# Retention, experts and a cosine MLP in one kernel: the places of tokens in stages of one chunk each, with the column comparison on POOL

## The chip, the cores and the metric

The kernel runs on one core of a Trainium2 chip. The metric is the time of one execution in microseconds (us) on the device; several runs are given by their median. The engines are called as in the profile: PE is TensorE, DVE is VectorE, ACT is ScalarE, POOL is GpSimd, SP is SyncE, which issues most of the transfers.

## What is computed

The batch is 8, with 8 heads, 576 positions and a head size of 64, so 4608 tokens of 512 numbers. All is float32.

```python
# retention: q, k, v are (8, 8, 576, 64)
scores = q @ k^T / 8
ret = scores * where(rel >= 0, gamma[h] ** rel, 0)      # rel = row - column
x = (ret @ v), heads put side by side                   # 4608 x 512
# mixture of 8 experts, one per token
logits = x @ w_gate                                     # 512 x 8
e = argmax(logits);  gate = softmax(logits)[e]          # sum + 1e-9
y = gate * (relu(x @ w1[e]) @ w2[e])                    # 1024 wide
# MLP with a cosine gate
h = y @ w_in                                            # 2048 wide
out = (h * cos(h)) @ w_out
```

## The kernel before

The kernel has three stages: retention together with the routing of the tokens, then the experts one after the other on the tokens gathered for each, then the MLP. The change is in the first stage alone.

The first stage goes through 40 steps, one chunk of a sequence each (`steps`, `CH`: four chunks of 128 tokens and one of 64 for each of the 8 sequences). The recording is manual: each engine executes its instructions in the order in which the program's text issues them. One pass of the loop over `i` (L497 on) issues work of several steps:

- `transposes(i + 1)`, `scores(i)`, `decay_k(i + 2)`, then in passes 20 to 27 `unit_split`, which splits one half unit of expert 0's weights into two parts on ACT and DVE (its load was issued two passes earlier by `unit_load`),
- `inter(i - 1)` and `intra(i - 1)`: the product with the carried state, the product of masked scores (`pT`) and v, the state's update,
- `table` for the groups that are due, `place` for the group that was routed in the pass before, `rows(i - 2)`, and `route` where a group is complete,
- the loads of step `i + 4` on SP, behind the store of the rows (`xd`).

`rows` (L335) makes the tokens' rows and the router's logits in one product, copies the rows on ACT and reduces the logits (`lgt`) on DVE at L344. Its PSUM tile has the tag of the scores' tile, "sc", in a pool with one buffer:

```python
two = ps1.tile([P, 8, P], F32, tag="sc", name="sc")     # L290, scores
two = ps1.tile([P, 8, P], F32, tag="sc", name="rw")     # L338, rows (then rearranged)
```

So the scores of the next step wait until `lgt` has read the tile, and the products of `rows` wait until both halves of `pT` have.

The routing works on groups of chunks (`groups`, L476): five chunks for each of the first seven sequences, and 2, 1 and 2 for the last. `route` (L351) finds each token's expert: five small DVE instructions. `place` (L369) does all that follows but the table: the ranks of the tokens within their experts by small products on PE with `rsb`, the counts so far; the slot `dst`; a comparison of the slot with the first slot of each of the 40 columns of 128 slots (`dd`, `ge`, `hot`, L396 to L401); the slot within its column (`rm`); one-hot rows over 128 slots (`oh`) and three rows of values (`rt`) on POOL; the gates (`gates`); and the new counts (`rsum`, `rsb`). `ve` is POOL, or DVE for the last group (`last`). `table` (L450) adds products of `oh` and `rt` to a table in SBUF that lists the tokens of each slot. It follows `place` by two passes.

Of the kernel before, what the change touches and what calls it, by code (L numbers as in the profile page):

```python
# [11 lines left out]
F32 = mybir.dt.float32  # L12
# [5 lines left out]
ALU = mybir.AluOpType  # L18
AX = mybir.AxisListType
# [3 lines left out]
P = 128  # L23
# [3 lines left out]
E = 8  # L27
# [3 lines left out]
CH = [(0, 128), (128, 128), (256, 128), (384, 128), (512, 64)]  # L31
# [72 lines left out]
def attn_moe_kernel(ctx, tc, q, k, v, wg, w1, w2, win, wout, ctab, out):  # L104
    nc = tc.nc
# [22 lines left out]
    rsum = cp.tile([P, E], F32, name="rsum")  # L128
# [19 lines left out]
    SL = E * NBLK  # L148
# [43 lines left out]
    with ExitStack() as actx:  # L192
        ap1 = actx.enter_context(tc.tile_pool(name="ap1", bufs=1))
        ap2 = actx.enter_context(tc.tile_pool(name="ap2", bufs=2))
# [12 lines left out]
        rsb = ap1.tile([P, E], BF16, name="rsb")  # L207
# [39 lines left out]
        steps = [(b, c) for b in range(B) for c in range(NCH)]  # L247
# [87 lines left out]
        def rows(i):  # L335
            b, c = steps[i]
            o, n = CH[c]
            two = ps1.tile([P, 8, P], F32, tag="sc", name="rw").rearrange("p (j a) t -> p j (a t)", a=2)  # L338
            for j in range(4):
                mm(out=two[:, j, 0:RW], lhsT=xts[i % 3][:, j, :], rhs=wgi[:, j, :], start=(j % 2 == 0), stop=True,  # L340
                   skip_group_check=True)
            x = ap3.tile([P, 4, P], F32, tag="xs", name="xs")
            nc.scalar.copy(out=x[:n], in_=two[:n, :, 0:P])
            nc.vector.tensor_reduce(out=lgt[b % 2][:n, c, :], in_=two[:n, :, P:RW].rearrange("p j e -> p e j"),  # L344
                                    axis=AX.X, op=ALU.add)
            nc.sync.dma_start(out=xd[b * SEQ + o:b * SEQ + o + n, :], in_=x[:n].rearrange("p j t -> p (j t)"))
# [22 lines left out]
        def place(i0, n, ohb, df):  # L369
            c0 = steps[i0][1]  # L370
            sh = [P, n, E]
            ex = ap2.tile(sh, F32, tag="ex", name="ex")
# [9 lines left out]
            for c in range(n - 1):  # L382
                m = n - 1 - c
                mm(out=rk[:, c + 1:, :], lhsT=ones, rhs=ohb[:, c, :].unsqueeze(1).to_broadcast([P, m, E]),
                   start=False, stop=(c == n - 2), skip_group_check=True)
            last = i0 + n == NS
            t1 = ap2.tile(sh, F32, tag="t1", name="t1")
            nc.vector.tensor_mul(out=t1, in0=rk, in1=ohb)
            dst = dsts[:, i0:i0 + n]
            nc.vector.tensor_reduce(out=dst, in_=t1, axis=AX.X, op=ALU.add)  # L390

            ve = nc.vector if last else nc.gpsimd
            hs = [P, n, SL]
            lo = cc(C_LO, SL).unsqueeze(1).to_broadcast(hs)
            dd = ap2.tile(hs, F32, tag="dd", name="dd")
            nc.vector.tensor_tensor(out=dd, in0=dst.unsqueeze(2).to_broadcast(hs), in1=lo, op=ALU.subtract)  # L396
            ge = ap2.tile(hs, F32, tag="ge", name="ge")
            nc.vector.tensor_scalar(out=ge, in0=dd, scalar1=0.0, scalar2=None, op0=ALU.is_ge)
            hot = ap2.tile(hs, F32, tag="hot", name="hot")
            nc.vector.scalar_tensor_tensor(out=hot, in0=dd, scalar=float(P), in1=ge, op0=ALU.is_lt, op1=ALU.mult)  # L400
            ve.tensor_tensor(out=dd, in0=dd, in1=hot, op=ALU.mult)  # L401
            rm = ap2.tile([P, n], F32, tag="rm", name="rm")
            nc.vector.tensor_reduce(out=rm, in_=dd, axis=AX.X, op=ALU.add)
            rt = ap2.tile([P, n, 3, SL], F32R, tag="rt", name="rt")
# [4 lines left out]
            for c in range(n):  # L409
                ve.tensor_scalar(out=oh[:, c, :], in0=cc(C_IOTA, P), scalar1=rm[:, c:c + 1], scalar2=None,  # L410
                                 op0=ALU.is_equal)
# [14 lines left out]

            if not last:
                gates()
            if n > 2:
                rr = ap2.tile([P, E], F32, tag="rr", name="rr")  # L430
                nc.vector.tensor_reduce(out=rr, in_=ohb[:, :n - 1].rearrange("p c e -> p e c"), axis=AX.X, op=ALU.add)
                nc.vector.tensor_add(out=rsum, in0=rsum, in1=rr)
            elif n == 2:
                nc.vector.tensor_add(out=rsum, in0=rsum, in1=ohb[:, 0, :])
            m = CH[c0 + n - 1][1]
            nc.vector.tensor_add(out=rsum[:m], in0=rsum[:m], in1=ohb[:m, n - 1, :])
            nc.vector.tensor_copy(out=rsb, in_=rsum)

            def enter(k0, k1):
                w = (k1 - k0) * SL  # L440
# [26 lines left out]
        groups[NS - 3] = (NS - 3, 1)  # L467
        groups[NS - 1] = (NS - 2, 2)
        routed = []
        tabled = []  # L470

        load(0, "q")
# [22 lines left out]
        for i in range(NS + 5):  # L495
            if i + 1 < NS:
                transposes(i + 1)  # L497
            if i < NS:
                scores(i)
            if i + 2 < NS:  # L500
                decay_k(i + 2)
            if 20 <= i < 20 + len(wq):
                unit_split(*wq[i - 20], upA)
            if i == 0:
                setup()
            if 1 <= i <= NS:
                inter(i - 1)
                intra(i - 1)

            prev, waiting[:], tabled[:] = waiting[:], tabled[:], []  # L510
            for r in prev:
                table(*r)
            if i >= NS + 2:
                while waiting:
                    table(*waiting.pop(0))
            prev, routed[:] = routed[:], []
            for r in prev:
                place(*r)
            if 0 <= i - 2 < NS:
                rows(i - 2)  # L520
            if i - 2 in groups:
                route(*groups[i - 2])
            if i + 4 < NS:
                loads(i + 4)
            if 18 <= i < 18 + len(wq):
                unit_load(ap3, *wq[i - 18])

        assert not tabled and not routed and not waiting
        assert not tabled and not routed
        rp = ps2.tile([P, 512], F32, tag="x", name="xps")  # L530
        mm(out=rp[:, :E], lhsT=ones, rhs=rsb, start=True, stop=True)
# [503 lines left out]
```

## Time and profile before

| | |
|---|---|
| time, median of 3 runs | 1568.36 us (1565.32 to 1570.71) |
| the profiled execution: time, span | 1571.7 us, 1569.8 us |
| mean granted clock of PE | 0.971 |
| PE busy | 1502.7 us, 96% of the span |
| DVE, ACT, POOL busy | 896.1, 781.1, 359.3 us |
| stage one | the first 291 us or so of the span |

The times of the rows further down are in us from the start of the span. A row of the timeline merges like instructions that follow each other ("x16" is their number), and in square brackets stands the idle time of the engine ahead of them, with what ended it. The granted clock is a share of 2.4 GHz: 1.00 is that level, 0.50 is the lower one of 1.2 GHz, and a value between is a mean over the stretch.

### The profile page before, as it was taken

To read this page: it belongs to the slowest core of one execution; us is meant where nothing else is said; L and a number is where in the kernel's file an instruction comes from. 1 tells how busy PE (TensorE), PEld (TensorE's weight loads), DVE (VectorE), ACT (ScalarE), POOL (GpSimd) and SP (SyncE) were. 2 spreads that over 40 slices of the span, in tenths; PEclk is the share of its full clock that TensorE was granted. 3 is DMA by queue.
4 is the path that set the end of the run, shared out by engine and by line. 5 is a ranking of instruction groups with operands and counts; after the bars stand their busy time and mean duration, and the time that the engine had idled before them with its cause. 6 is when DMAs were issued, how large, how long until landed. Compare 5 with 4: busy or idle time off the path is not lost.

```text
span 1569.8 us, 24472 instructions
## 1 busy us (share of the span) xinstructions
PE 1502.7 (96%) x9565; PEld 1334.4 (85%) x9565; DVE 896.1 (57%) x1618; ACT 781.1 (50%) x1395; POOL 359.3 (23%) x399
## 2 busy tenths in 40 slices
PE   8997798799999999999999999999999999999998
PEld 7887788699999999999878888888888888888886
DVE  3555655556575665652256656666665656666554
ACT  3334332244445445433266666666565666666654
POOL 3111111365666657562000101010000101010101
PEclk9999899699999999999999999999999999999999
DMA  9768763365657556556640100000010100000000
GB/s 184 161 146 186 182 136 88 104 203 190 201 188 226 195 182 237 180 162 213 218 162 28 48 7 34 21 27 28 1 53 1 54 1 28 0 27 1 28 0 27
DMA packets 168520, 163.10 MB, mean 104 GB/s; under 512 B 119012, under 2 KB 127664, under 8 KB 166352
## 3 DMA queue, kind: packets, MB, share of 16 engines
q1 hardware_dynamic: 155696, 110.50, 25.8%
q0 software_dynamic: 10688, 36.31, 6.6%
q10 hardware_dynamic: 2016, 14.68, 2.8%
q8 instruction: 76, 1.25, 0.3%
q14 instruction: 44, 0.36, 0.1%
HBM read 115.70 MB, written 45.76 MB: 103 GB/s over the span
## 4 chain that ended last, share of the span: by engine, by line
issue 42%; PE 4%; POOL 2%; ACT 1%; DVE 1%; DMA 0%; POOLq 0%; SPq 0%
PE hps L907 2%; POOL out_dram L959 2%; PE acc L949 1%; PE acc L951 1%; PE acc L950 1%; DVE sa L918 0%; ACT ka L915 0%; DVE sa L919 0%; ACT sa L921 0%; ACT sa L922 0%; POOL spare L140 0%; DVE ka L917 0%; DMA yin<-ydT 0%; ACT sa L923 0%; DVE gl L934 0%
## 5 line engine op out<-in xcount | busy, mean ns | idle before, releaser
L907 PE MATMUL hps<-yT,wunit 128*128 128x512 f32 x1728 | 417.5, 391 | 0.4 <-ACT yT L894 0.4
L907 PEld LDWEIGHTS hps<-yT,wunit 128*128 128x128 f32 x1728 | 324.9, 188 | 69.8 <-DVE yT L895 1.3
L949 PE MATMUL acc<-wunit,gh 128*128 128x512 f32 x576 | 224.1, 389 | 0.0
L950 PE MATMUL acc<-wunit,gh 128*128 128x512 f32 x576 | 224.1, 389 | 0.0
L951 PE MATMUL acc<-wunit,gl 128*128 128x512 f32 x576 | 224.1, 389 | 0.0
L621 PE MATMUL hps<-hh,wunit 128*128 128x360 f32 (+1 forms) x1024 | 223.6, 310 | 0.0
L606 PE MATMUL hps<-xT,wunit 128*128 128x360 f32 (+1 forms) x1536 | 222.8, 306 | 0.5 <-ACT xT L591 0.5
L606 PEld LDWEIGHTS hps<-xT,wunit 128*128 128x128 f32 x1536 | 220.6, 190 | 1.2 <-ACT xT L591 0.9
L959 POOL DMA_INDIRECT out_dram<-orow,perm x36 | 35.2, 978 | 808.7 <-DVE orow L955 802.3
L929 DVE TENSOR_TENSOR sa<-hps,sa 128x512 f32<-128x512 f32 x144 | 99.3, 690 | 160.2 <-ACT sa L923 160.2
L921 ACT ACTIVATE sa<-sa 128x512 f32<-128x512 f32 x144 | 91.1, 633 | 193.8 <-DVE sa L919 193.8
L698 POOL TENSOR_TENSOR wunit<-wst,wunit 128x512 fp32r<-128x512 f32 x112 | 157.6, 1426 | 89.6 <-ACT wunit L697 89.4
L621 PEld LDWEIGHTS hps<-hh,wunit 128*128 128x128 f32 x1024 | 172.1, 192 | 0.0
L621 PE MATMUL hps<-hl,wunit 128*128 128x360 f32 (+1 forms) x512 | 158.1, 309 | 4.8 <-DVE hl L610 4.8
L610 DVE SCALAR_TENSOR_TENSOR hl<-hps,hh 128x360 fp32r<-128x360 f32 (+1 forms) x128 | 60.6, 474 | 178.1 <-ACT hh L609 178.1
L915 ACT ACTIVATE ka<-hps,biases 128x512 f32<-128x512 f32 x144 | 99.0, 688 | 69.4 <-PE hps L907 69.4
L951 PEld LDWEIGHTS acc<-wunit,gl 128*128 128x128 f32 x576 | 108.2, 188 | 22.5
L950 PEld LDWEIGHTS acc<-wunit,gh 128*128 128x128 f32 x576 | 108.1, 188 | 22.5
L949 PEld LDWEIGHTS acc<-wunit,gh 128*128 128x128 f32 x576 | 108.2, 188 | 22.4
L623 ACT COPY yev<-hps 128x256 f32<-128x256 f32 (+1 forms) x64 | 26.7, 417 | 169.1 <-issue 93.9
L923 ACT ACTIVATE sa<-sa,biases 128x512 f32<-128x512 f32 x144 | 104.1, 723 | 4.7
L917 DVE TENSOR_SCALAR ka<-ka 128x512 f32<-128x512 f32 x144 | 61.0, 424 | 74.2 <-ACT ka L915 74.2
(148 smaller groups left out, 2055.5 us busy)
## 6 DMA issues: line engine op xcount, KB each, us to landing
wst<-in_moe_w_dram SPq DMA_DIRECT2D x64, 512.0 KB, 4.5
wd<-cvo POOLq DMA_DIRECT2D x32, 512.0 KB, 3.9
wunit<-wd ACTq DMA_DIRECT2D x14, 1024.0 KB, 5.9
yin<-ydT SPq DMA_DIRECT2D x36, 256.0 KB, 2.7
ldq<-in_q_dram SPq DMA_DIRECT2D x32, 256.0 KB, 3.5
ldk<-in_k_dram SPq DMA_DIRECT2D x32, 256.0 KB, 4.2
ldv<-in_v_dram SPq DMA_DIRECT2D x32, 256.0 KB, 4.5
xd<-xs SPq DMA_DIRECT2D x32, 256.0 KB, 2.2
```

Source lines behind the costliest of these rows:

```text
L606: mm(out=ph[:, :n], lhsT=u[:, a, kc, f0:f0 + P], rhs=t[:, bq, kc, :n], start=(idx == 0), stop=(idx == 11))
L621: mm(out=py[:, :n], lhsT=u[:, w], rhs=t[:, :n], start=(fc == 0 and g == 0), stop=(fc == 7 and g == 2))
L698: nc.gpsimd.tensor_sub(out=u[:, 1, 2 * g + c], in0=s[:, c], in1=u[:, 0, 2 * g + c])
L907: mm(out=ph, lhsT=u[:, a, kc, f0:f0 + P], rhs=t[:, bq, kc, :], start=(idx == 0), stop=(idx == 11))
L915: nc.scalar.activation(out=ka, in_=ph, func=AF.Identity, scale=INV2PI, bias=magic)
L921: nc.scalar.activation(out=sa, in_=sa, func=AF.Sin, scale=0.5)
L923: nc.scalar.activation(out=sa, in_=sa, func=AF.Identity, scale=-2.0, bias=one)
L929: nc.vector.tensor_mul(out=sa, in0=ph, in1=sa)
L949: mm(out=a, lhsT=gh[:, s], rhs=u[:, 0, fc % 4], start=(fc == 0), stop=False)
L950: mm(out=a, lhsT=gh[:, s], rhs=u[:, 1, fc % 4], start=False, stop=False)
L951: mm(out=a, lhsT=gl[:, s], rhs=u[:, 0, fc % 4], start=False, stop=(fc == 15))
L959: ins = nc.gpsimd.indirect_dma_start(out=out[:, :], out_offset=bass.IndirectOffsetOnAxis(ap=perm[:, k:k + 1], axis=0), in_=o, in_offset=None)
```

## The change

`place` is cut in two. What is left in `place` is the ranks, the slot, the comparison and the new counts. The rest, from `rm` on, is a new function `spread`, with the gates in it. For a group that isn't the last, `spread` runs one pass later, and `table` so two passes after that. For the last group `place` calls it at once, in the old order.

For groups that aren't the last the comparison (`dd`, `ge`, `hot`) moves from DVE to POOL; the instruction that made `hot` becomes two there. In the loop, `rows` comes ahead of `spread` and `place`, and so does `route`.

```diff
@@ -393,12 +393,35 @@
             hs = [P, n, SL]
             lo = cc(C_LO, SL).unsqueeze(1).to_broadcast(hs)
             dd = ap2.tile(hs, F32, tag="dd", name="dd")
-            nc.vector.tensor_tensor(out=dd, in0=dst.unsqueeze(2).to_broadcast(hs), in1=lo, op=ALU.subtract)
+            ve.tensor_tensor(out=dd, in0=dst.unsqueeze(2).to_broadcast(hs), in1=lo, op=ALU.subtract)
             ge = ap2.tile(hs, F32, tag="ge", name="ge")
-            nc.vector.tensor_scalar(out=ge, in0=dd, scalar1=0.0, scalar2=None, op0=ALU.is_ge)
+            ve.tensor_scalar(out=ge, in0=dd, scalar1=0.0, scalar2=None, op0=ALU.is_ge)
             hot = ap2.tile(hs, F32, tag="hot", name="hot")
-            nc.vector.scalar_tensor_tensor(out=hot, in0=dd, scalar=float(P), in1=ge, op0=ALU.is_lt, op1=ALU.mult)
+            if last:
+                ve.scalar_tensor_tensor(out=hot, in0=dd, scalar=float(P), in1=ge, op0=ALU.is_lt, op1=ALU.mult)
+            else:
+                ve.tensor_scalar(out=hot, in0=dd, scalar1=float(P), scalar2=None, op0=ALU.is_lt)
+                ve.tensor_tensor(out=hot, in0=hot, in1=ge, op=ALU.mult)
             ve.tensor_tensor(out=dd, in0=dd, in1=hot, op=ALU.mult)
+            if last:
+                spread(i0, n, ex, hot, dd, True)
+            if n > 2:
+                rr = ap2.tile([P, E], F32, tag="rr", name="rr")
+                nc.vector.tensor_reduce(out=rr, in_=ohb[:, :n - 1].rearrange("p c e -> p e c"), axis=AX.X, op=ALU.add)
+                nc.vector.tensor_add(out=rsum, in0=rsum, in1=rr)
+            elif n == 2:
+                nc.vector.tensor_add(out=rsum, in0=rsum, in1=ohb[:, 0, :])
+            m = CH[c0 + n - 1][1]
+            nc.vector.tensor_add(out=rsum[:m], in0=rsum[:m], in1=ohb[:m, n - 1, :])
+            nc.vector.tensor_copy(out=rsb, in_=rsum)
+            if not last:
+                placed.append((i0, n, ex, hot, dd, False))
+
+        def spread(i0, n, ex, hot, dd, last):
+
+            c0 = steps[i0][1]
+            hs = [P, n, SL]
+            ve = nc.vector if last else nc.gpsimd
             rm = ap2.tile([P, n], F32, tag="rm", name="rm")
             nc.vector.tensor_reduce(out=rm, in_=dd, axis=AX.X, op=ALU.add)
             rt = ap2.tile([P, n, 3, SL], F32R, tag="rt", name="rt")
@@ -426,15 +449,6 @@
 
             if not last:
                 gates()
-            if n > 2:
-                rr = ap2.tile([P, E], F32, tag="rr", name="rr")
-                nc.vector.tensor_reduce(out=rr, in_=ohb[:, :n - 1].rearrange("p c e -> p e c"), axis=AX.X, op=ALU.add)
-                nc.vector.tensor_add(out=rsum, in0=rsum, in1=rr)
-            elif n == 2:
-                nc.vector.tensor_add(out=rsum, in0=rsum, in1=ohb[:, 0, :])
-            m = CH[c0 + n - 1][1]
-            nc.vector.tensor_add(out=rsum[:m], in0=rsum[:m], in1=ohb[:m, n - 1, :])
-            nc.vector.tensor_copy(out=rsb, in_=rsum)
 
             def enter(k0, k1):
                 w = (k1 - k0) * SL
@@ -467,6 +481,7 @@
         groups[NS - 3] = (NS - 3, 1)
         groups[NS - 1] = (NS - 2, 2)
         routed = []
+        placed = []
         tabled = []
 
         load(0, "q")
@@ -513,19 +528,22 @@
             if i >= NS + 2:
                 while waiting:
                     table(*waiting.pop(0))
-            prev, routed[:] = routed[:], []
-            for r in prev:
-                place(*r)
             if 0 <= i - 2 < NS:
                 rows(i - 2)
+            to_spread, placed[:] = placed[:], []
+            to_place, routed[:] = routed[:], []
             if i - 2 in groups:
                 route(*groups[i - 2])
+            for r in to_spread:
+                spread(*r)
+            for r in to_place:
+                place(*r)
             if i + 4 < NS:
                 loads(i + 4)
             if 18 <= i < 18 + len(wq):
                 unit_load(ap3, *wq[i - 18])
 
-        assert not tabled and not routed and not waiting
+        assert not tabled and not routed and not waiting and not placed
         assert not tabled and not routed
         rp = ps2.tile([P, 512], F32, tag="x", name="xps")
         mm(out=rp[:, :E], lhsT=ones, rhs=rsb, start=True, stop=True)
```

What the change moves, at three places. `ohb` is a token's expert as a one-hot row, `t` the ranks masked by it, `lg` the PSUM tile of ranks and table, `rw` the PSUM tile of `rows`.

DVE, first group of five chunks, from the middle of `place` to the next step's `pT`. Before:

```order
L403 TENSOR_REDUCE rm<-dd 128x5
L416 TENSOR_REDUCE gts<-ex 128x5
L417 TENSOR_SCALAR gts<-gts 128x5
L418 RECIPROCAL gts<-gts 128x5
L421 CAST gh<-gts 128x5
L422 TENSOR_TENSOR gl<-gts,gh 128x5
L431 TENSOR_REDUCE rr<-ohb 128x8
L432 TENSOR_TENSOR rsum<-rsum,rr 128x8
L436 TENSOR_TENSOR rsum<-rsum,ohb 64x8
L437 CAST rsb<-rsum 128x8
L344 TENSOR_REDUCE lgt_135<-rw 128x8
L299 TENSOR_TENSOR pT<-sc,ca 128x4x128 x2
```

Ahead of these stand L388, L390, L396, L398 and L400, which are t, dsts and the comparison. Now, from the end of the step's `intra`:

```order
L325 TENSOR_TENSOR xt_123<-xps,gx 128x512
L344 TENSOR_REDUCE lgt_135<-rw 128x8
L388 TENSOR_TENSOR t_728<-lg,ohb 128x40
L390 TENSOR_REDUCE dsts<-t_728 128x5
L410 TENSOR_REDUCE rr<-ohb 128x8
L411 TENSOR_TENSOR rsum<-rsum,rr 128x8
L415 TENSOR_TENSOR rsum<-rsum,ohb 64x8
L416 CAST rsb<-rsum 128x8
L299 TENSOR_TENSOR pT<-sc,ca 128x4x128 x2
```

`lgt` has moved from behind fifteen instructions of `place` to directly behind `xt`; the comparison has gone; rm and the gates (now L426 and L439 to L445) stand one step further down, behind the next `lgt` and ahead of the `pT` of the 64-token chunk.

POOL, one group of five chunks. Before:

```order
L401 TENSOR_TENSOR dd<-dd,hot 128x200
L406 TENSOR_SCALAR tokc<-ct 128x5
L407 TENSOR_TENSOR rt<-hot,tokc 128x5x40
L410 TENSOR_SCALAR oh<-ca,rm 128x128 x5
L424 TENSOR_TENSOR rt<-hot,gh 128x5x40
L424 TENSOR_TENSOR rt<-hot,gl 128x5x40
```

Now:

```order
L396 TENSOR_TENSOR dd<-dsts,ca 128x200
L398 TENSOR_SCALAR ge<-dd 128x200
L403 TENSOR_SCALAR hot<-dd 128x200
L404 TENSOR_TENSOR hot<-hot,ge 128x200
L405 TENSOR_TENSOR dd<-dd,hot 128x200
L429 TENSOR_SCALAR tokc<-ct 128x5
L430 TENSOR_TENSOR rt<-hot,tokc 128x5x40
L433 TENSOR_SCALAR oh<-ca,rm 128x128 x5
L447 TENSOR_TENSOR rt<-hot,gh 128x5x40
L447 TENSOR_TENSOR rt<-hot,gl 128x5x40
```

Four instructions on 128x200 have come ahead of the product that was POOL's first.

PE, the end of the stage, from the ranks of the group of one chunk to those of the last group; the rows of the difference, where L458 is the table's line L444 under its new number:

```order
 L380 LDWEIGHTS tri
 L380 MATMUL lg<-ohb,tri 128x8
-L340 MATMUL rw<-wgi,xt_127 128x136 x4
-L444 MATMUL lg<-rt,oh 128x120 x2
 L340 MATMUL rw<-wgi,xt_123 128x136 x4
-L444 MATMUL lg<-rt,oh 128x120
+L458 MATMUL lg<-rt,oh 128x120 x3
 L376 LDWEIGHTS ones
 L376 MATMUL lg<-rbase,ones 128x16
```

The rows of the last chunk but one go ahead of these ranks (further up), and the tables of the last two groups ahead of the last ranks stand together behind the products of the last rows.

In the steps with `place`, the products of `rows` (L340) also stand ahead of the rank products (L376 to L384) on PE, and on ACT the copy of the rows (L343) ahead of `ex` (L373). SP's order is unchanged, and so is all that follows the stage on every engine.

## Rows read from the trace of the kernel before

**Rows 1.** Two stretches of the attention stage. Columns: the stretch in us, its length, then the busy time and number of instructions of PE, weight loads, DVE, ACT and POOL, the granted clock, the mean busy share of the DMA engines, and GB/s.

```profile
84.00:117.00 33.00, 29.82 (x354) 26.90 (x352) 17.44 (x47) 10.55 (x25) 5.25 (x10) 0.90 0.63 144
...
153.00:191.00 38.00, 31.00 (x350) 27.98 (x349) 22.60 (x52) 15.47 (x29) 5.25 (x10) 0.87 0.82 192
```

**Rows 2.** The waits between 20 and 260 us: who waited for whom, us in total, how often, the longest.

```profile
DVE lgt L344 <- ACT xs L343: 32.4, 25, 1.8
PE sc L295 <- DVE lgt L344: 28.5, 12, 3.7
...
ACT wunit L179 <- DMA wst<-in_moe_w_dram: 14.2, 6, 4.8
```

**Rows 3.** PE's timeline: the scores (L295) of the seven steps that follow a `place` of five chunks, each with the products of `rows` (L340) that end its step, and a step without such a wait (249.05 to 254.77). Columns: start, length, engine, line, operation, tiles, shapes, number, and the idle time ahead.

```profile
57.11 1.83 PE L295 MATMUL sc<-qT,kpT 64*128 64x128 f32 x16 [3.05 <-DVE lgt L344]
...
62.37 1.19 PE L340 MATMUL rw<-wgi,xt 128*128 128x136 f32 x8
...
88.88 2.08 PE L295 MATMUL sc<-qT,kpT 64*128 64x128 f32 x16 [3.03 <-DVE lgt L344]
...
95.36 1.19 PE L340 MATMUL rw<-wgi,xt 128*128 128x136 f32 x8
...
121.86 1.74 PE L295 MATMUL sc<-qT,kpT 64*128 64x128 f32 x16 [3.02 <-DVE lgt L344]
...
127.08 1.19 PE L340 MATMUL rw<-wgi,xt 128*128 128x136 f32 x8
...
158.18 1.16 PE L295 MATMUL sc<-qT,kpT 64*128 64x128 f32 x16 [3.03 <-DVE lgt L344]
...
163.44 1.19 PE L340 MATMUL rw<-wgi,xt 128*128 128x136 f32 x8
...
196.29 1.16 PE L295 MATMUL sc<-qT,kpT 64*128 64x128 f32 x16 [3.03 <-DVE lgt L344]
...
201.54 1.19 PE L340 MATMUL rw<-wgi,xt 128*128 128x136 f32 x8
...
228.04 2.08 PE L295 MATMUL sc<-qT,kpT 64*128 64x128 f32 x16 [3.03 <-DVE lgt L344]
...
233.30 1.19 PE L340 MATMUL rw<-wgi,xt 128*128 128x136 f32 x8
...
249.05 1.17 PE L340 MATMUL rw<-wgi,xt 128*128 128x136 f32 x8
...
251.10 1.16 PE L295 MATMUL sc<-qT,kpT 64*128 64x128 f32 x16
...
254.77 0.19 PE L376 MATMUL lg<-rbase,ones 128*128 128x40 bf16 x1
...
259.79 2.08 PE L295 MATMUL sc<-qT,kpT 64*128 64x128 f32 x16 [3.02 <-DVE lgt L344]
...
266.17 1.19 PE L340 MATMUL rw<-wgi,xt 128*128 128x136 f32 x8
```

**Rows 4.** The timeline of DVE, and one row of POOL, around the seventh `place`: the step before it (250.86 to 252.31) and the `place` itself.

```profile
250.86 0.18 DVE L344 TENSOR_REDUCE lgt<-rw 64x8 f32<-64x32 f32 x1 [0.76 <-ACT xs L343]
...
252.01 0.20 DVE L366 TENSOR_TENSOR ohb<-rsc,m 128x40 bf16<-128x40 f32 x1
...
252.31 1.29 DVE L299 TENSOR_TENSOR pT<-sc,ca 128x512 f32<-128x512 f32 x2
...
255.14 0.20 DVE L388 TENSOR_TENSOR t<-lg,ohb 128x40 f32<-128x40 f32 x1
...
255.37 0.20 DVE L390 TENSOR_REDUCE dsts<-t 128x5 f32<-128x40 f32 x1
...
257.38 0.36 DVE L403 TENSOR_REDUCE rm<-dd 128x5 f32<-128x200 f32 x1 [0.72 <-POOL dd L401]
...
257.76 0.52 POOL L407 TENSOR_TENSOR rt<-hot,tokc 128x200 fp32r<-128x200 f32 x1
257.88 0.42 DVE L417 TENSOR_SCALAR gts<-gts 128x5 f32<-128x5 f32 x1
...
258.77 0.17 DVE L422 TENSOR_TENSOR gl<-gts,gh 128x5 fp32r<-128x5 f32 x1
...
259.55 0.18 DVE L344 TENSOR_REDUCE lgt<-rw 128x8 f32<-128x32 f32 x1
```

**Rows 5.** Instructions grouped by line and shape, from 0 to 290 us. Columns: line, engine, operation, tiles, shapes, number, busy us and mean ns of one, then the idle time ahead of them and what ended it.

```profile
L410 POOL TENSOR_SCALAR oh<-ca,rm 128x128 fp32r<-128x128 f32 x38 | 22.3, 603 | 0.0
...
L180 DVE TENSOR_TENSOR wunit<-wst,wunit 128x1024 fp32r<-128x1024 f32 x8 | 9.7, 1218 | 6.2 <-ACT wunit L179 6.2
...
L401 POOL TENSOR_TENSOR dd<-dd,hot 128x200 f32<-128x200 f32 x7 | 4.2, 607 | 201.5 <-DVE hot L400 201.5
...
L406 POOL TENSOR_SCALAR tokc<-ct 128x5 f32<-128x5 f32 x7 | 1.7, 239 | 0.6
```

**Rows 6.** Two stretches of 6 us, columns as in rows 1: behind the third `place`, and where weights of expert 0 are loaded.

```profile
123.00:129.00 6.00, 6.00 (x62) 5.39 (x60) 2.65 (x5) 1.43 (x4) 1.23 (x3) 0.78 0.31 54
...
141.00:147.00 6.00, 4.30 (x62) 3.83 (x60) 2.97 (x4) 2.11 (x4) 0.00 (x0) 1.00 1.11 250
```

**Rows 7.** PE's timeline near the end of the stage: the last products of `rows`, and the first rank product of the last group.

```profile
280.83 2.18 PE L340 MATMUL rw<-wgi,xt 128*128 128x136 f32 x8 [1.72 <-DVE lgt L344]
...
285.15 0.17 PE L376 MATMUL lg<-rbase,ones 128*128 128x16 bf16 x1 [2.05 <-DVE tab L453]
```

## The prediction

> **What bounds the kernel now.** I read the stretches first. In the attention stage TensorE is the engine to watch: in a stretch of 33 us it is busy for 29.82, VectorE for 17.44, and the granted clock is 0.90 [rows 1]. The stage has 40 steps, one chunk of 128 (or 64) tokens each, so what a step costs is what TensorE waits in it. The waits come second: inside 20 to 260 us, TensorE's scores wait 28.5 us in all for one small VectorE instruction, the reduction of the router's logits (`lgt`, L344), and the longest is 3.7 us [rows 2]. Third, TensorE's timeline gives these waits their places. Seven of them, of 3.02 to 3.05 us, stand in the seven steps in which `place` handles five chunks [rows 3]; I number them places 1 to 7.
>
> VectorE's timeline around place 7 says why [rows 4]. The logits' products share one PSUM tile with the scores, so the next scores can't be written before `lgt` has read them. On VectorE `lgt` stands behind all of `place`: from 255.14 to 259.55 us, 4.4 us of fifteen small instructions and a wait of 0.72 for POOL. In the step before, nothing stands ahead of `lgt`: the logits' products start at 249.05, `lgt` runs from 250.86 to 251.04, and the scores start at 251.10 [rows 3, 4], 2.05 us after the products and without an idle time shown.
>
> The wait has a second price. After it the scores take 1.74 to 2.08 us at five of the seven places, where they take 1.16 in an undisturbed step [rows 3]; in 123 to 129 us, which follows place 3, the granted clock is 0.78 though TensorE is busy all the time [rows 6]. TensorE goes at its lower level, 1.2 in place of 2.4 GHz, for some microseconds after each idle stretch of 3 us.
>
> **The change, part by part.**
>
> *Logits' products ahead of `place`.* In VectorE's order `lgt` now comes first and the rank instructions follow. TensorE's wait at each place should fall to what other steps have. What is removed: 3.05 + 3.03 + 3.02 + 3.03 + 3.03 + 3.03 + 3.02 = **21.2 us** of waits [rows 3].
>
> *The low clock behind them.* From the start of the scores to the products behind the step's last attention matmul, an undisturbed step takes 254.77 - 251.10 = 3.67 us. After places 1 to 7 the same work takes 5.26, 6.48, 5.22, 5.26, 5.25, 5.26 and 6.38 [rows 3]. Less seven times 3.67 that is **13.4 us**. It goes if no other idle time of that length takes the wait's place.
>
> *What now stands between `lgt` and the masking of the scores (`pT`) in the place step.* Six instructions: t and dsts (255.14 to 255.57, 0.43) and rr to rsb (0.78 between the starts of gl at 258.77 and `lgt` at 259.55) [rows 4], 1.2 us. `pT` has to wait for the scores anyway: in the routing step five instructions lie in the same gap, ending at 252.21, and `pT` starts at 252.31. So the cover is the scores' own time. If it fails, `pT` ends at 253.60, and the next products that need its PSUM tile come at 254.77: 1.2 us more of slack. Cost: nothing.
>
> *The one-hot rows and gates one step later (`spread`).* Six VectorE instructions from rm at 257.38 to the end of gl, 1.56 us [rows 4], now lie behind `lgt` and ahead of the next `pT`, which is that of a 64-row chunk. That `pT` starts about 0.8 us later than now, and it is half as long; its products are due 3.2 us after its scores start (an estimate from 3.67, with half a microsecond less for the short scores). It ends some 2.3 us after they start. Cost: nothing, with 0.9 us left.
>
> *The comparison on POOL.* Three VectorE instructions become four on POOL, ahead of the product that POOL has already. No row shows a compare of 128x200 on POOL. From below: the 128x128 compare at 0.603 us. From above: 0.603 x 200/128 = 0.94. Between 128x5 (0.239) and 128x128 the slope gives 0.82 for 200, which I take, since it is the same kind of instruction. The chain is then 3 x 0.607 + 2 x 0.82 and four gaps of some 0.1 us: 3.9 us, between 3.4 and 4.1 [rows 5]. It starts after dsts, 0.4 us behind the scores' start, and rm wants it behind the next `lgt`, which ends 3.67 + (251.04 - 249.05) = 5.66 us behind that start [rows 3, 4]: 5.3 us. The 0.72 us that rm waits for POOL now is inside what is already counted. With 1.4 us to spare, and 0.9 more of slack at `pT`, the chain costs nothing; past some 6.2 us it would.
>
> *The table one step later.* Its five products move from a step with a 128-row chunk to one with a 64-row chunk and cost the same there. One-hot rows (five at 0.603) and gate rows are done two steps ahead of it. Cost: nothing. SP's order of transfers does not change; each xd store gets its rows earlier in seven steps.
>
> *Place 4 gives back.* It lies where expert 0's weights are loaded and split, in steps 20 to 27. ScalarE already waits 14.2 us there for these transfers [rows 2], and the DMA share reaches 1.11 at 250 GB/s [rows 6]. Over 153 to 191 us it is 0.82 [rows 1]. When place 4's 3.03 + 1.59 = 4.6 us go, transfers that those microseconds had covered are late next. Also VectorE carries a 1.22 us weight subtraction per step there [rows 5] and has less slack. The loss lies between 0 and 4.6; I take **3.0**, nearer the upper end, since a DMA share of 0.82 would become 0.93 if nothing waited. For small waits left at the six other places I take **0.8** (0.1 each, more at place 3).
>
> *The end of the stage.* The last three groups follow each other closely. TensorE waits 1.72 us for `lgt` and 2.05 for the table there [rows 7]. Putting `lgt` first takes most of the former; but the group before last now needs POOL's longer chain, ahead of the last table but one. Following both orders with the durations above, the last ranks come some 0.8 us earlier; the bounds are 2.5 earlier (most of both waits) and 2 later (the second one doubled). I take **0.8**. All behind it is the same work in the same order, bounded by TensorE, so the gain is carried to the end.
>
> Sum: 21.2 + 13.4 - 3.0 - 0.8 + 0.8 = **31.6 us**. The profiled execution took 1571.7 us (its span 1569.8 and 1.9 around it), so the same execution would take 1540.1. The median of the runs is 3.3 below it, and so the forecast is **1537 us**.
>
> **The rivals.**
>
> *The two engines hold each other up.* During POOL's chain VectorE has four instructions with two SBUF operands or of the copy kind: two sums into rsum, rsb, and the next kp. Speaking for it: a VectorE instruction on 128x5 takes 0.42 us at 257.88 and ends 0.02 after a POOL product that began before it, where its neighbour gl takes 0.17 [rows 4]. Against: gl itself reads two such operands, and 0.17 us is all it takes at 258.77, beside the one-hot rows that POOL makes after that product. If each of the four waits out a POOL instruction of 0.6 to 0.8, that is 2.4 to 3.2 us against 1.2 of slack, so 1.2 to 2.0 us lost at each of seven places, 8 to 14 in all: 1545 to 1551 us. The Trainium skill states this as a rule (SBUF — State Buffer, Who interferes with whom): a VectorE instruction that reads two SBUF operands, or runs in a two-port mode, and a GpSimd instruction that reads SBUF exclude each other for the whole instruction. By that rule, the 0.42 us row agrees and gl's row does not.
>
> *DMA takes back more.* Places 3 and 4 both give all their 3.02 + 1.55 + 3.03 + 1.59 = 9.2 us to weights that are still on their way: 31.6 + 3.0 - 9.2 = 25.4 us gained, 1543 us. Against it: place 3 ends ahead of the weight transfers, at a share of 0.31 [rows 6].
>
> *POOL becomes the wait* (slower). rm heads VectorE's queue in the next step and waits for POOL's last product. It costs from a chain of 6.2 us on, and the time comes out longer than before once the new wait passes the old one of 3.03 us, so from 9.2 us on. At three times the rows (11.7 us) the wait is 5.5 us, with 2.7 of low clock behind it, as at place 2; a place costs (21.2 + 13.4)/7 = 4.9 us now, so 3.3 us more, 23 in all: 1591 us. Four new compares on two broadcast operands, which no row shows, speak for it; 0.607 and 0.603 us speak against [rows 5].
>
> *The wait only changes its name* (same). `lgt` also waits for ScalarE's copy of the rows, 32.4 us in all [rows 2]. If that copy is what comes last at the places too, the scores wait on, and the time stays at 1568 us. Against: at 250.86 it holds `lgt` for 0.76 us, and the scores behind it still show no idle time [rows 3, 4].
>
> **How the numbers follow.** The forecast as summed gets 0.76, the mutual hold-up 0.10, DMA 0.08, POOL 0.03, the changed name 0.03. The sum's own bounds are 31.6 + 3.0 + 1.7 = 36.3 us and 31.6 - 1.6 - 2.8 = 27.2 us, 1532 to 1541; two microseconds for the spread of runs (1565.32 to 1570.71) go on the fast side. On the slow side the range takes in the second rival and all but the worst of the first. Range **1529 to 1550 us**. About 0.3% (4.7 us) is what a measurement of this kernel can tell from no change. The first three cases are all faster by more: 0.94. Same 0.03, slower 0.03.
>
> **What would show it.** Right: in the places the scores wait under 0.5 us for `lgt` and take 1.16; the granted clock is 1.00 through 50 to 130 us; POOL's chain takes 3.4 to 4.2 us and rm hardly waits; weights waited for 2 to 5 us longer in all. Wrong: a wait of 1 us or more at `pT` or the products behind it in the place step (first rival), a wait of rm on POOL (third), or waits of 3 us that are still there under another name.

## The result

The changed kernel takes **1532.88 us** (median of 4 runs, 1530.69 to 1533.75) where the kernel before took 1568.92 in the same comparison (1565.32 to 1570.71): ratio 0.977, 95% interval 0.975 to 0.979, so 36.0 us less. The forecast was 1537.0 us, in 1529 to 1550.

The profiled execution of the changed kernel took 1530.69 us, the lowest of its runs, and its span is 1528.9 us; the profiled one of before (1571.7) lay 2.8 us above its median. So the two spans differ by 40.9 us, five more than the medians do, and what is added up from these two traces below belongs to the 40.9.

The same two stretches as in [rows 1], then the two as in [rows 6], and all of 20 to 240 us, in the changed kernel. Columns as there.

```profile
84.00:117.00 33.00, 32.67 (x438) 29.56 (x434) 20.26 (x56) 12.72 (x29) 13.44 (x22) 1.00 0.79 176
153.00:191.00 38.00, 35.74 (x459) 32.22 (x461) 24.72 (x59) 17.25 (x35) 8.81 (x14) 1.00 0.85 194
123.00:129.00 6.00, 4.96 (x67) 4.50 (x67) 3.56 (x7) 2.61 (x4) 0.00 (x0) 1.00 1.15 277
141.00:147.00 6.00, 5.96 (x84) 5.35 (x85) 5.63 (x14) 2.71 (x6) 5.67 (x8) 1.00 0.96 240
20.00:240.00 220.00, 209.24 (x2711) 188.80 (x2707) 136.65 (x351) 88.26 (x195) 68.54 (x112) 1.00 0.77 177
```

And 20 to 240 us of the kernel before:

```profile
20.00:240.00 220.00, 193.77 (x2329) 174.66 (x2324) 122.90 (x301) 77.93 (x168) 34.25 (x65) 0.92 0.73 163
```

The granted clock is 1.00 in the whole stretch, where it was 0.92. TensorE is busy for 15 us more of the same 220 us, and gets through 2711 matmul instructions instead of 2329. The stage ends earlier, and behind it nothing changes: from VectorE's first instruction on the last group's ranks (L388) to the end, 1284.4 us went by before (1569.8 - 285.44) and 1283.9 now (1528.9 - 245.01).

The waits between 20 and 240 us, to hold against [rows 2]:

```profile
DVE lgt L344 <- ACT xs L343: 44.3, 34, 1.5
...
ACT wunit L179 <- DMA wst<-in_moe_w_dram: 19.0, 8, 4.3
PE sc L295 <- DVE lgt L344: 7.8, 10, 2.4
```

The scores wait 7.8 us in all for `lgt`, where they waited 25.4 us in the same 220 us before (28.5 in [rows 2], whose stretch is 20 us longer and takes in place 7). ScalarE waits longer for the weights, 19.0 us against 14.2, as the forecast had it; what that does is told further down.

TensorE at places 1, 2 and 7, to hold against [rows 3]:

```profile
53.79 1.16 PE L295 MATMUL sc<-qT,kpT 64*128 64x128 f32 x16 [0.15 <-DVE lgt L344]
...
57.46 1.19 PE L340 MATMUL rw<-wgi,xt 128*128 128x136 f32 x8
...
81.06 1.16 PE L295 MATMUL sc<-qT,kpT 64*128 64x128 f32 x16 [0.15 <-DVE lgt L344]
...
84.73 1.19 PE L340 MATMUL rw<-wgi,xt 128*128 128x136 f32 x8
...
223.44 1.16 PE L295 MATMUL sc<-qT,kpT 64*128 64x128 f32 x16
...
227.10 1.19 PE L340 MATMUL rw<-wgi,xt 128*128 128x136 f32 x8
```

Each of the seven places now has scores of 1.16 us and a wait of 0.15 us or none. From the scores to the products of `rows` it takes 3.66 or 3.67 us at the three shown (57.46 - 53.79), the length of a step without a wait, 3.67. The scores that took 2.08 us at places 2 and 7 before were the same 16 matmuls at the lower clock (granted clock 0.50 from 90 to 92 and from 260 to 262 us).

VectorE and POOL around place 1, to hold against [rows 4] (a row's line numbers are those of the changed kernel):

```profile
54.22 0.48 DVE L411 TENSOR_TENSOR rsum<-rsum,rr 128x8 f32<-128x8 f32 x1
...
55.06 1.27 DVE L299 TENSOR_TENSOR pT<-sc,ca 128x512 f32<-128x512 f32 x2
56.25 0.68 DVE L269 TENSOR_TENSOR kp<-ldk,ca 128x512 f32<-128x512 f32 x1
...
59.31 0.19 DVE L344 TENSOR_REDUCE lgt<-rw 128x8 f32<-128x32 f32 x1 [1.51 <-ACT xs L343]
59.42 0.35 DVE L426 TENSOR_REDUCE rm<-dd 128x5 f32<-128x200 f32 x1
```

```profile
54.15 0.52 POOL L396 TENSOR_TENSOR dd<-dsts,ca 128x200 f32<-128x200 f32 x1 [31.73 <-DVE dsts L390]
54.77 0.71 POOL L398 TENSOR_SCALAR ge<-dd 128x200 f32<-128x200 f32 x1
55.45 0.72 POOL L403 TENSOR_SCALAR hot<-dd 128x200 f32<-128x200 f32 x1
56.25 1.15 POOL L404 TENSOR_TENSOR hot<-hot,ge 128x200 f32<-128x200 f32 x1
57.48 0.60 POOL L405 TENSOR_TENSOR dd<-dd,hot 128x200 f32<-128x200 f32 x1
```

POOL's chain takes 3.93 us here (54.15 to 58.08), and `rm` needs it at 59.42. So 1.3 us are to spare; at place 4, where the chain is longest, 0.5 us are (144.13 to 144.60). No wait of `rm` for POOL is listed between 20 and 240 us.

### The profile page after: what moved, and what is told of

Same layout as the page of the kernel before. It is cut to its first block, busy times and chain, and to the rows that moved or that the text cites. A ratio compares the mean times of both kernels' runs of the same rounds, so it can differ in the third digit from the quotient of the medians.

```text
span 1528.9 us, 24475 instructions
## 1 busy us (share of the span) xinstructions
PE 1481.8 (97%) x9565; PEld 1315.5 (86%) x9565; DVE 890.6 (58%) x1591; ACT 780.1 (51%) x1395; POOL 387.1 (25%) x435
## 4 chain that ended last, share of the span: by engine, by line
issue 43%; PE 4%; POOL 2%; ACT 1%; DVE 1%; DMA 0%; POOLq 0%; SPq 0%
PE hps L925 2%; POOL out_dram L977 2%; PE acc L969 1%; PE acc L967 1%; PE acc L968 1%; DVE sa L936 0%; ACT ka L933 0%; DVE sa L937 0%; ACT sa L939 0%; ACT sa L940 0%; POOL spare L140 0%; DVE ka L935 0%; DMA yin<-ydT 0%; ACT sa L941 0%; DVE gl L952 0%
```

## The experiments

Eleven kernels besides the two. "Before" and "after" are the two kernels of this document; times are medians, and every ratio is to the kernel before in the same comparison.

| kernel | edit | us | ratio, 95% interval |
|---|---|---|---|
| after | the whole change | 1532.9 | 0.977 (0.975 to 0.979) |
| e1 | before + new order alone | 1552.8 | 0.990 (0.988 to 0.991) |
| e4 | before + comparison on POOL alone | 1581.0 | 1.007 (1.005 to 1.009) |
| e2 | after, `place` ahead of `rows` again | 1534.2 | 0.977 (0.975 to 0.979) |
| e3 | after, comparison on VectorE again | 1532.3 | 0.976 (0.975 to 0.978) |
| e10 | both undone: the split alone | 1543.2 | 0.983 (0.982 to 0.984) |
| e5 | before + TensorE kept busy in the wait | 1552.8 | 0.989 (0.987 to 0.990) |
| e6a | after, POOL's chain 2.8 us longer | 1535.7 | 0.978 (0.976 to 0.980) |
| e6b | after, POOL's chain 6.9 us longer | 1573.3 | 1.002 (1.001 to 1.003) |
| e9 | before, weight loads spread | 1559.2 | 0.994 (0.992 to 0.995) |
| e7 | after, weight loads spread | 1525.2 | 0.971 (0.970 to 0.973) |
| e8 | e7 and e3 together | 1525.9 | 0.972 (0.971 to 0.974) |

**e1: the order alone.** In the kernel before:

```diff
-            prev, routed[:] = routed[:], []
-            for r in prev:
-                place(*r)
             if 0 <= i - 2 < NS:
                 rows(i - 2)
+            prev, routed[:] = routed[:], []
             if i - 2 in groups:
                 route(*groups[i - 2])
+            for r in prev:
+                place(*r)
```

Expected: 

> The kernel before with rows and route ahead of place, nothing else moved. Theory A (what counts is how soon lgt follows its products, and how late pT may come): lgt is no longer late, but 4.4 us of place now stand between lgt and pT, 3.2 us more than the scores cover; pT has 1.2 us of slack, so TensorE waits some 2.0 us at each place with no lasting low clock: a place costs 2.0 in place of 4.9 us, 1544 to 1549 us. Rival (the order of rows and place is the whole gain): 1533 to 1535 us.

Measured: 17.1 us less, under half of the change. The wait moved as theory A said. TensorE behind place 2:

```profile
85.17 1.16 PE L295 MATMUL sc<-qT,kpT 64*128 64x128 f32 x16 [0.15 <-DVE lgt L344]
...
90.88 1.17 PE L340 MATMUL rw<-wgi,xt 128*128 128x136 f32 x8 [1.97 <-DVE pT L299]
91.88 0.95 PE L279 MATMUL tp<-ct,ldq 128*128 128x128 f32 x4
```

The scores wait 0.15 us; the whole of `place` now stands between `lgt` and `pT`, and the products that need `pT`'s tile wait 1.97 us. From 92 to 97 us the granted clock is 0.66. A had expected no lasting low clock behind 2 us. It follows at five of the seven places; at places 4 and 5, with the same wait of 1.97 us, the granted clock is 1.00 behind it (153.6 to 158.0 and 184.7 to 189.0 us). A's 1544 to 1549 missed by 4 us. It had not counted, either, on the waits for `lgt` among the weights, which shrink from 7.0 to 3.2 us with no low clock behind them. At the places, the order alone turns one wait into a shorter one with another name.

**e4: the comparison on POOL alone.** In the kernel before:

```diff
-            nc.vector.tensor_tensor(out=dd, ...)
+            ve.tensor_tensor(out=dd, ...)
...
-            nc.vector.tensor_scalar(out=ge, ...)
+            ve.tensor_scalar(out=ge, ...)
...
-            nc.vector.scalar_tensor_tensor(out=hot, ...)
+            if last:
+                ve.scalar_tensor_tensor(out=hot, ...)
+            else:
+                ve.tensor_scalar(out=hot, ..., op0=ALU.is_lt)
+                ve.tensor_tensor(out=hot, in0=hot, in1=ge, op=ALU.mult)
```

Expected: 

> The kernel before with the comparison on POOL, nothing else moved. Theory A: VectorE waits for POOL's chain of 3.4 us in the middle of place, lgt comes 1.6 us later at seven places, the low clock lasts longer: 1580 to 1586 us. Rival (VectorE relieved of 1.1 us per group): 1561 us.

Measured: 11.2 us slower, as A had it. The waits between 20 and 240 us say how:

```profile
PE sc L295 <- DVE lgt L344: 35.2, 11, 5.4
...
DVE rm L407 <- POOL dd L405: 21.0, 6, 3.5
```

With `rm` still in the same step, VectorE waits 3.5 us for POOL, and `lgt` waits behind it. Work taken off VectorE made VectorE later.

**e2, e3 and e10: what of the change is needed.** e2 puts the call of `place` ahead of `rows` again, in the changed kernel; e3 puts the comparison back on VectorE in three instructions (the lines of e4's diff, the other way); e10 does both, so that only the split of `place` into two steps is left. The diff of e2, in the changed kernel:

```diff
+            for r in to_place:
+                place(*r)
             if 0 <= i - 2 < NS:
                 rows(i - 2)
...
-            for r in to_place:
-                place(*r)
```

Expected of e2: 

> The changed kernel with place ahead of rows again (split and comparison on POOL kept). Theory A: the six instructions left in place end before the products and the copy of the rows do, so lgt is not late: 1533 us, within 2. Rival (rows ahead of place is what counts): lgt comes 0.5 to 1 us later at seven places, 1537 to 1540 us.

Expected of e3: 

> The changed kernel with the comparison back on VectorE (split and order kept). Theory A: 1.1 us more between lgt and pT, which has 1.2 us of slack: 1533 to 1535 us. Rival (VectorE's time is what the change frees): 1.1 us more at seven places, 1541 us.

Expected of e10: 

> The changed kernel with place ahead of rows (as e2) and the comparison on VectorE (as e3) together: of the change only the split into two steps is left. In e2 the eight logits' scores waited 0.30 us at the first place, lgt having ended 0.05 us before them; three comparison instructions on VectorE take 1.07 us there (85.49 to 86.56 in e1) and lgt waits 0.19 us for ScalarE in e2. Theory A (either of the two other parts is cover enough alone, but one of them is needed): lgt ends 0.9 us later, the scores wait 1.2 us at each of seven places, no low clock behind: 6 us over e2 and e3, 1538 to 1542 us. Rival (the split is all the change): 1531 to 1535 us. Third way (waits of 1.2 us bring the low clock back): 1545 us or more.

Measured: e2 and e3 are where the changed kernel is (intervals that overlap almost wholly), as theory A of each had it, e3 0.7 us below A's range. e10 is 9 to 11 us behind them. Its TensorE at place 1:

```profile
55.54 1.16 PE L295 MATMUL sc<-qT,kpT 64*128 64x128 f32 x16 [1.15 <-DVE lgt L344]
```

That is the 1.2 us expected, and it stands at six of the seven places as 1.14 or 1.15 (1.84 at the fifth, among the weights). The time, 1543.2 us, is 1.2 us above A's range. One weight wait was followed by low clock, which neither e3 nor the changed kernel had there (e2 had it, behind a wait of 2.55 us):

```profile
136.88 2.08 PE L295 MATMUL sc<-qT,kpT 64*128 64x128 f32 x16 [2.73 <-DVE lgt L344]
```

So the split carries the change (e10 has 26.2 us of the 36), and either of the other two parts supplies the cover for what is left; the second one then adds nothing. The other two parts together without the split were not run.

**e5: the low clock as a cost of its own.** In the kernel before, 24 idle bf16 products on TensorE ahead of the scores that wait; they write a part of a PSUM tile that nothing reads.

```diff
+            fill[:] = [rp] if n == NCH else []
...
+            if fill:
+                t = ident.bitcast(BF16)
+                bank = fill.pop()
+                for _ in range(24):
+                    mm(out=bank[:, 256:512], lhsT=t[:, :P], rhs=t, ...)
             if i < NS:
```

Expected: 

> The kernel before with 24 idle products of 256 columns on TensorE ahead of the scores that wait at each place (about 2.6 us at the full clock, inside the wait of 3.03 us; their result is not used). Theory A: the waits stay, the slow scores behind them go: 13.4 us less than before, 1555 us, within 3. Rival (the matmuls there are slow from something else that goes on at the time, not from the idle time): 1569 us.

Measured: 17.1 us less, with the wait itself still there:

```profile
55.33 2.79 PE L504 MATMUL lg<-ct 128*128 128x256 bf16 x24
58.46 1.16 PE L295 MATMUL sc<-qT,kpT 64*128 64x128 f32 x16 [0.33 <-DVE lgt L344]
...
62.13 1.19 PE L340 MATMUL rw<-wgi,xt 128*128 128x136 f32 x8
```

The scores come no earlier, but take 1.16 us, and the step behind them 3.67. This is the second price of the prediction by itself, 13.4 us in its sum. The 17.1 measured hold more than that, since TensorE also lost less among the weights, where it has no fill:

```profile
143.21 1.16 PE L295 MATMUL sc<-qT,kpT 64*128 64x128 f32 x16 [2.93 <-DVE lgt L344]
...
175.91 1.84 PE L295 MATMUL sc<-qT,kpT 64*128 64x128 f32 x16 [1.86 <-DVE lgt L344]
```

With 0.7 us more at place 4 these are 5.5 us of waits, with 1.6 us of low clock behind the second; before, it was 7.0 us with 4.1 us of low clock (the lines are in the next section).

**e6a and e6b: POOL's chain made longer.** In the changed kernel POOL's last product is made five or eleven times over.

```diff
-            ve.tensor_tensor(out=dd, in0=dd, in1=hot, op=ALU.mult)
+            for _ in range(1 if n < NCH else 5):   # e6b: 11
+                ve.tensor_tensor(out=dd, in0=dd, in1=hot, op=ALU.mult)
```

Expected of e6a: 

> The changed kernel with POOL's last product of the comparison made four times more (the result is the same): POOL's chain takes 6.2 us in place of 3.4. Theory A: this is where it begins to cost, 1533 to 1535 us. Rival (each microsecond of POOL's chain counts): 2.8 us at seven places, 1552 us.

Expected of e6b: 

> The changed kernel with POOL's last product of the comparison made ten times more: a chain of 10.3 us. Theory A: rm waits some 5 us at the head of VectorE's queue, 0.9 us of it covered, and the low clock returns: 6 to 6.8 us at seven places, 1575 to 1581 us, slower than before. Rival (POOL is off the path at any length): 1533 us.

Measured: with a chain of 6.7 us at place 1 (55.06 to 61.74) e6a is 2.8 us behind the changed kernel. The two intervals overlap, so the time alone does not show a loss; in the trace `rm` waits 9.1 us in all, and TensorE's products of `rows` wait 3.9 us for `pT`, which they do nowhere in the changed kernel. With a chain of 10.8 us (54.45 to 65.27) e6b is 40 us behind and 0.2% slower than the kernel before. Both came out by theory A's mechanism and just outside its ranges, e6a 0.7 us above 1533 to 1535, e6b 1.8 us below 1575 to 1581. In e6b at place 1 the wait passes from VectorE to TensorE:

```profile
65.30 0.36 DVE L427 TENSOR_REDUCE rm<-dd 128x5 f32<-128x200 f32 x1 [5.51 <-POOL dd L406]
```

```profile
67.67 2.15 PE L340 MATMUL rw<-wgi,xt 128*128 128x136 f32 x8 [4.56 <-DVE pT L299]
```

So "POOL becomes the wait" is what happens with a longer chain. It costs little at 6.7 us, which agrees with the prediction's 6.2 as the start. The chain at which the change gains nothing lies between 6.7 and 10.8 us; a straight line between the two puts it at 10.4 (an estimate), where 9.2 was forecast. The changed kernel's 3.9 us is far from it.

**e9, e7, e8: the weights.** Expert 0's eight half-unit loads are issued in passes 5, 9, ... 33 and split three passes later, in place of passes 18 to 25 and 20 to 27. e9 does it to the kernel before, e7 to the changed one, e8 is e7 with e3's edit.

```diff
-            if 20 <= i < 20 + len(wq):
-                unit_split(*wq[i - 20], upA)
+            if 8 <= i < 8 + 4 * len(wq) and i % 4 == 0:
+                unit_split(*wq[i // 4 - 2], upA)
...
-            if 18 <= i < 18 + len(wq):
-                unit_load(ap3, *wq[i - 18])
+            if 5 <= i < 5 + 4 * len(wq) and i % 4 == 1:
+                unit_load(ap3, *wq[i // 4 - 1])
```

Expected of e7: 

> The changed kernel with expert 0's eight half units loaded every fourth pass from pass 5 and split three passes later, in place of eight passes in a row. Theory A (what is left of waits in steps 20 to 27 is transfers that come too close together): 6.2 us of TensorE's waits go, 1527 us, within 2. Rival (the transfers are late wherever they stand, or push others): 1533 us or more.

Expected of e9: 

> The kernel before, with expert 0's half-unit loads spread over passes 5 to 33 as in e7; nothing else changed. This weighs the forecast's term for the weights (the waits of the places cover some of the transfers, so the changed order would lose 3.0 us there). Theory A: the weights' waits and the low clock behind them simply stand beside those of the places, and nothing is covered: before, they are 7.0 us of waits and 4.1 us of low clock (6.2 and none in the changed kernel), so spreading takes 9 to 11 us off: 1558 to 1560 us. Rival (the forecast's reason): the places cover 3 us of the transfers in the kernel before, so spreading brings 3 us less here than the 7.7 us that it brought in the changed kernel: 1564 us. If spreading brings the same in both kernels: 1561 us.

Expected of e8: 

> The changed kernel with e7's spread loads and e3's comparison on VectorE together. Theory A (the comparison costs nothing on either engine once lgt stands ahead of it): within 1.5 us of e7's 1525.2. Rival (with the weights out of the way VectorE's 1.4 us more per place show up on the path): 1530 or more.

Measured: e9 is 10.0 us under the kernel before. That is within theory A's 1558 to 1560; its interval, 1557 to 1561.5, leaves room for "the same in both" (1561), and none for the forecast's reason (1564). e7 is 7.7 us under the changed kernel (from two comparisons, whose intervals to the kernel before lie apart), and e8 is level with e7. e7 and e8 beat both kernels. In e7 no wait of ScalarE for the weights is listed, and TensorE in the stretch in which they had been loaded is busy throughout at full clock:

```profile
120.00:160.00 40.00, 39.59 (x499) 35.52 (x498) 25.26 (x63) 17.71 (x37) 10.63 (x15) 1.00 0.84 196
```

Without the weights' waits the change is worth 1559.2 - 1525.2 = 34.0 us, against 21.2 + 13.4 + 0.8 - 0.8 = 34.6 in the forecast's terms for all but the weights. The measure is not quite clean. At places 2 and 6 of e9 a weight subtraction of 1.21 us now stands ahead of `place` on VectorE, and the scores wait 1.4 us more in all than before:

```profile
89.46 2.08 PE L295 MATMUL sc<-qT,kpT 64*128 64x128 f32 x16 [3.72 <-DVE lgt L344]
```

Less these, the places and the end of the stage are worth 32.6 us.

## Why the prediction was right, step by step

*Waits at the places, 21.2 us:* right. 0.15 us is left at places 1, 2 and 5 and nothing at the other four, 0.45 us in all where the sum had set 0.8 aside. e1 shows that `lgt`'s place in VectorE's order is what made them.

*Low clock, 13.4 us:* right, and e5 shows that it is a price of its own, which goes while the wait stays. With the 21.2 it makes 34.6, close to the 34.0 us (or 32.6) by which e9 and e7 differ. The prediction's "after each idle stretch of 3 us" holds for its seven places and not everywhere, as the last section shows.

*What stands between `lgt` and `pT`, nothing:* right in the changed kernel, and the cover is thinner than the sum assumed. At place 1 `pT` starts at 55.06 us, and the scores end at 53.79 + 1.16 = 54.95. e1 shows the price when it fails: 2 us of wait at each place.

*`spread` and the table one step later, nothing:* right. In the step behind place 1 the 64-row `pT` ends 1.95 us after its scores start (59.56 to 61.51), 2.3 in the prediction, and the products that wait for it come at 3.18 us (62.74). No wait of TensorE is listed there or at the table's products (67.58 us).

*Place 4 gives back 3.0 us:* **wrong: nothing was given back.** The step that failed is "transfers that those microseconds had covered are late next". Before, TensorE waited 0.51 + 2.59 + 0.20 + 3.71 = 7.0 us for `lgt` behind the weights, and two of those waits had low clock behind them:

```profile
147.88 1.16 PE L295 MATMUL sc<-qT,kpT 64*128 64x128 f32 x16 [2.59 <-DVE lgt L344]
153.15 0.19 PE L376 MATMUL lg<-rbase,ones 128*128 128x40 bf16 x1
...
185.06 2.08 PE L295 MATMUL sc<-qT,kpT 64*128 64x128 f32 x16 [3.71 <-DVE lgt L344]
191.26 0.19 PE L376 MATMUL lg<-rbase,ones 128*128 128x40 bf16 x1
```

with 5.27 and 6.20 us to the products behind the step's last attention matmul, where a step at full clock takes 3.67: 4.1 us of low clock. After, the waits of this stretch are

```profile
126.08 1.16 PE L295 MATMUL sc<-qT,kpT 64*128 64x128 f32 x16 [1.04 <-DVE lgt L344]
...
133.16 1.16 PE L295 MATMUL sc<-qT,kpT 64*128 64x128 f32 x16 [2.40 <-DVE lgt L344]
...
136.83 1.19 PE L340 MATMUL rw<-wgi,xt 128*128 128x136 f32 x8
...
150.80 1.16 PE L295 MATMUL sc<-qT,kpT 64*128 64x128 f32 x16 [0.80 <-DVE lgt L344]
...
157.08 1.16 PE L295 MATMUL sc<-qT,kpT 64*128 64x128 f32 x16 [0.64 <-DVE lgt L344]
...
163.08 1.16 PE L295 MATMUL sc<-qT,kpT 64*128 64x128 f32 x16 [1.31 <-DVE lgt L344]
```

6.2 us, and none is followed by low clock (3.67 us from 133.16 to 136.83). ScalarE's wait for the transfers did grow, by 4.8 us, as forecast, but TensorE's did not: five waits of 0.6 to 2.4 us stand where 2.6 and 3.7 were the largest. By these two traces the term is a gain of 0.8 us of waits and 4.1 of low clock, outside the 0 to 4.6 us of loss that the prediction allowed.

A single trace is thin ground for that. It is of the fastest of the changed kernel's four executions, with a mean granted clock of 0.987 where the other three had 0.984. But eight more traces have the loads in the same passes (e1 to e6b and e10). Their waits there add up to 3.1 to 6.8 us, never to more than the 7.0 of before, and low clock follows one of them at most. By the medians, the weights cost 10.0 us before (e9; 11.4 with the 1.4 us that the spread itself cost there) and 7.7 after (e7): a gain of 2.3 to 3.7 us, from differences that have intervals of 2 to 3 us each. So the size stays open, between 2 and 5 us of gain; a loss of 3.0 is in none of these figures.

Why the waits came out smaller stays open too. More idle time on VectorE ahead of `lgt`, in which a late split can be taken, cannot be the whole reason: they are 3.2 us in e1 and 5.5 in e5, where VectorE does all that it did before. A swing from a loss of 3.0 to a gain of 2 or more is what lies between the 31.6 us forecast and the 36.0 measured. The forecast held in spite of this sign because the term is small beside the places'.

*The end of the stage, 0.8 us:* right in sign, about 1.4. `lgt` of the step behind place 7 starts 39.07 us earlier (268.02 to 228.95), the last group's ranks 40.43 (285.44 to 245.01). TensorE's waits there have new names, against [rows 7]:

```profile
238.60 1.19 PE L340 MATMUL rw<-wgi,xt 128*128 128x136 f32 x8 [0.89 <-DVE lgt L344]
240.60 0.43 PE L458 MATMUL lg<-rt,oh 128*128 128x120 f32 x2 [0.80 <-DVE rsb L416]
243.88 0.47 PE L458 MATMUL lg<-rt,oh 128*128 128x120 f32 x1 [2.84 <-POOL rt L447]
```

*The comparison on POOL, 3.9 us a chain:* right at five of the seven places (3.93 or 3.94; 4.81 at place 4, 3.40 at place 7), though by errors that cancel. The compare took 0.71 us, not 0.82; the product behind it took 1.15 us in place of 0.61 where VectorE made `kp` at the same time.

*The rival of the two engines:* the mechanism is there, its price is not. The sum into `rsum` that starts at 54.22 us takes 0.48 and ends at 54.70, behind POOL's subtraction of 54.15 (to 54.67). In e1 it takes 0.17, at 88.98 us, beside POOL's one-hot rows. POOL's product of 56.25 takes 1.15 and ends 0.47 behind `kp`, which starts with it; at place 7, where no `kp` follows, it takes 0.61. So some 0.3 us on VectorE and 0.5 on POOL at a place, inside the slack of both: at the places of the changed kernel neither the products that need `pT`'s tile nor `rm` wait. e3 does not test this, since there POOL's one product holds up the same sum (0.56 us at 83.62). The rule of the Trainium skill that the prediction gives (SBUF — State Buffer, Who interferes with whom) agrees with these two pairs. It does not agree with `rsum` in e1 and `gl` in [rows 4], which take 0.17 us beside POOL's one-hot rows; in the changed kernel `gl` and the next `kp` take 0.1 us more beside them (0.30 at 60.55 and 0.80 at 61.44).

*DMA takes back more* and *the wait only changes its name:* neither. ScalarE's copy holds `lgt` oftener now (34 times, 44.3 us), but for 1.5 us at most, and at the places the scores behind it wait 0.15 us or not at all.

## What to carry to other kernels

A small instruction that frees a shared PSUM tile belongs ahead of every long piece on its engine, and the long piece is best cut so that the parts with distant consumers fall into the next step; the order alone moves two thirds of the wait to the next reader (e1, 1.97 of 3.03 us), and moving work to another engine without changing where its result is awaited can cost time (e4). When waits on TensorE are priced, price the low clock behind them too: here it was two thirds as much again (13.4 on 21.2), and it could be had back without shortening the wait at all (e5). Parts of a change that each cover the same gap are not worth their sum: look for the one that is enough.

## What the runs showed of the hardware

The length of a single wait did not tell whether the clock fell. It fell to 0.66 behind a wait of 1.86 us in e5 (176 to 181 us), behind 1.97 in e1, and to 2.08 us scores behind 2.73 in e10. It stayed at 1.00 behind 2.93 us in e5 (143 to 149 us), behind 2.40 in the changed kernel, behind two other waits of 1.97 in e1, and behind 3.08 us in e4 (153.9 to 158.9 us):

```profile
153.90 1.16 PE L295 MATMUL sc<-qT,kpT 64*128 64x128 f32 x16 [3.08 <-DVE lgt L344]
```

Before, behind places 4 and 5, the scores still took 1.16 us and the fall came a little later in the step [rows 3]. Which of the waits of 1.9 to 3.1 us are followed by a fall stays open.

A POOL product of two 128x200 operands was lengthened by a VectorE instruction beside it, as well as the other way about. At place 4 two of POOL's products meet `kp` and the weight subtraction:

```profile
141.42 1.16 POOL L404 TENSOR_TENSOR hot<-hot,ge 128x200 f32<-128x200 f32 x1
142.65 1.48 POOL L405 TENSOR_TENSOR dd<-dd,hot 128x200 f32<-128x200 f32 x1
```

```profile
141.43 0.68 DVE L269 TENSOR_TENSOR kp<-ldk,ca 128x512 f32<-128x512 f32 x1
142.03 1.63 DVE L180 TENSOR_TENSOR wunit<-wst,wunit 128x1024 fp32r<-128x1024 f32 x1
```

Each POOL product ends 0.47 us behind the VectorE instruction that it started beside (142.58 and 142.11; 144.13 and 143.66), and the subtraction, 1.22 us elsewhere [rows 5], takes 1.63.
